# Two MLPs behind a packed attention: the early second products of batches 0 to 3 computed plainly instead of by Strassen's seven products

## The chip, the cores and the metric

The kernel runs on one core of one Trainium2 chip. The metric is the device time of one execution in microseconds (us). Of the kernel before there are three timed runs: 1403.85, 1407.91 and 1408.93 us, so a median of 1407.91 us. A fourth execution was profiled; it took 1409.86 us, 1408.0 us of them between its first and its last instruction (the span). All durations below come from that execution.

The engines are named as in the profile: PE (matrix products; PEld is its weight loading, which runs beside the products), DVE, ACT and POOL (elementwise work), SP (issues the DMA transfers).

## The reference, cut to what matters

```
p_packed = softmax(p k^T / 8) v            # 32 packed rows for each of 64 (batch, head)
x  = softmax(q p_packed^T / 8) p_packed    # 8 batches x 576 tokens x 512
g, val = x @ w_gate, x @ w_val             # 512 -> 1536
x2 = (silu(g) * val) @ w_out               # 1536 -> 512
h  = x2 @ w_in                             # 512 -> 2048
out = bend(h) @ wo2                        # h where h >= 1, 0 where h <= -1, (h + 1)^2 / 4 between
```

All values are float32. The kernel carries each operand of its large products as a high and a low float16 half, so that one product of operands is three matmuls: low by high, high by low, high by high.

## The kernel before, in words

**Units and passes.** The first MLP is cut into eight batches of 576 tokens and six pairs of blocks of its hidden dimension (a pair is 256 of the 1536 hidden columns). One batch with one pair is a *unit*. A unit's first product (`Projected.step`) is 8 steps of 6 matmuls, 48 matmuls of 288 columns; ahead of it stands its packed-row product (`make_projection`), 24 narrow matmuls that multiply the 32 packed rows of each head with the gate and value weights. ACT applies silu to a step's result, DVE multiplies the value half onto it, and the unit's hidden values then lie in a buffer `h` as four quarters (two hidden blocks by two halves of the batch's tokens). 

The order of units is fixed by `PHASES`: batch 0 with pair 0, batch 0 with pair 1, batch 1 with pairs 0 and 1, batches 0 and 1 with pair 2, batches 2 to 5 with pairs 0 to 2 each; after that pairs 3 to 5 of all eight batches, and pairs 0 to 2 of batches 6 and 7. One batch with one such group of pairs is a *pass*. The first twelve units make seven passes, those of batches 0 to 3 with pairs 0 to 2.

**The second product of a pass.** `second_strassen` multiplies the 2x2 blocks of the output weights with the 2x2 blocks of hidden values by Strassen's seven products. For that, `Projected.quarters` makes three sums and differences more and one intermediate from the four quarters and splits all seven operands into halves: four additions (three instructions), three casts to float16 and three subtractions for the low halves. Each of the seven products is done for both column groups of the output: 7 x 2 x 3 = 42 matmuls of 288 columns for a pair. The products are summed up in three PSUM banks for each group, and a bank is read after each of the seven into one of four accumulators, so there are 14 reads for a pass (`gather`, `add_to`; DVE, or ACT when the accumulator is fresh). A batch's accumulators are loaded from and stored to `sums1` in HBM between its passes. 

**Around it.** In the same stretch the kernel computes the attention, four heads of one batch at a time (a *quad*; 16 in all, in stages a, b and c), and converts the weights from float64 words (`convert_w1`, `prepare_w1`).

**What sets the order.** The kernel records every operation with its costs, its operands and the buffers it needs; `Order.run` then issues them to the engines by its own cost model, PE's in about the recorded sequence with a look ahead of 32 operations, the others by due times. On the chip each engine runs its list in that order and waits at semaphores. When a piece of attention or weight conversion is recorded is set by tables: two *places* go by in each unit, and `NEXT`, `REST` and `SPACE` name the places of quads 2 and later; `LATE` names those of the weights. `prepare(k + 1)` records the packed-row product of the next unit, at the start of unit k. There are 37 operand buffers `op` and eight PSUM banks, seven of them `ps`. Nearly every tensor operation of two inputs is recorded by one helper (`either`, L390), casts by another (`copy`, L402 to L408), every DMA by L433. Lines that the steps below speak of: L763 attention scores, L959 packed-row product, L1474 first product, L1417 second product, L1326 accumulation, L1484 silu, L1488 the value half, L647 and L652 the squares of the output weights and their sum over partitions.

## Time and profile before

| | |
|---|---|
| timed runs | 1403.85, 1407.91, 1408.93 us |
| profiled execution, its span | 1409.86 us, 1408.0 us |
| PE, PEld busy | 1339.7 us (95%), 1073.9 us (76%) |
| DVE, ACT, POOL busy | 1089.0 us (77%), 903.5 us (64%), 1092.9 us (78%) |
| unit 1 starts, unit 13 starts (first L1474 matmul) | 51.1 us, 251.9 us |
| second MLP starts (first L1205 matmul) | 718.5 us |

The busy time of PE is not its work at full speed: a matmul's span in the trace is longer than the distance to the next one when they follow closely, so a PE that is fed in bits can look busy. PEclk is the clock that PE was granted, 1.00 for 2.4 GHz; the other level is half of that.

### The profile page before, as it was taken

To read this page: it belongs to the slowest core of one execution; us is meant where nothing else is said; L and a number is where in the kernel's file an instruction comes from. 1 tells how busy PE (TensorE), PEld (TensorE's weight loads), DVE (VectorE), ACT (ScalarE), POOL (GpSimd) and SP (SyncE) were. 2 spreads that over 40 slices of the span, in tenths; PEclk is the share of its full clock that TensorE was granted. 3 is DMA by queue.
4 is the path that set the end of the run, shared out by engine and by line. 5 is a ranking of instruction groups with operands and counts; after the bars stand their busy time and mean duration, and the time that the engine had idled before them with its cause. 6 is when DMAs were issued, how large, how long until landed. Compare 5 with 4: busy or idle time off the path is not lost.

```text
span 1408.0 us, 33413 instructions
## 1 busy us (share of the span) xinstructions
PE 1339.7 (95%) x12903; PEld 1073.9 (76%) x12908; DVE 1089.0 (77%) x1985; ACT 903.5 (64%) x1663; POOL 1092.9 (78%) x936
## 2 busy tenths in 40 slices
PE   5788989899899999999999999999999999999998
PEld 2455656577576777777788888888888888888887
DVE  6998888897488887777878888777767878766774
ACT  5877776788477877777767566655545546564551
POOL 1468656678398988989998999987888979885883
PEclk8799999999999999999999999999999999999999
DMA  9865667677567777778865324352337531444312
GB/s 328 290 199 167 195 204 240 194 227 268 186 214 246 233 248 244 256 261 292 281 236 185 135 83 151 131 199 96 106 123 244 187 130 76 149 167 173 113 61 90
DMA packets 143455, 267.87 MB, mean 190 GB/s; under 512 B 15296, under 2 KB 77248, under 8 KB 143296
## 3 DMA queue, kind: packets, MB, share of 16 engines
q1 hardware_dynamic: 143296, 265.74, 56.6%
q8 instruction: 101, 1.65, 0.5%
q14 instruction: 58, 0.48, 0.1%
HBM read 168.30 MB, written 97.39 MB: 189 GB/s over the span
## 4 chain that ended last, share of the span: by engine, by line
PE 74%; POOL 3%; DVE 3%; DMA 2%; ACT 2%; issue 2%; SPq 0%; DVEq 0%; POOLq 0%; ACTq 0%
PE ps L1417 31%; PE ps L1205 20%; PE ps L1474 13%; PE cv L1417 4%; PE cv L1205 2%; PE ps L959 2%; POOL op L390 1%; DMA wsp<-raw 1%; PE ps L763 1%; DMA raw<-w2f 1%; POOL h L390 1%; POOL raw L390 1%; DVE acc L1326 0%; DMA op<-in_qT 0%; DMA raw<-in_wo 0%
## 5 line engine op out<-in xcount | busy, mean ns | idle before, releaser
L1417 PE MATMUL ps<-op,op 128*128 128x256 f16 (+1 forms) x4467 | 595.8, 279 | 19.3 <-POOL op L390 9.6
L1417 PEld LDWEIGHTS <-op 128*128 128x128 f16 x5040 | 492.1, 98 | 116.9 <-issue 29.4
L390 POOL TENSOR_TENSOR op<-h,op 128x512 f16<-128x512 f32 (+4 forms) x362 | 461.0, 1290 | 107.4 <-ACT op L402 88.1
L1474 PE MATMUL ps<-op,op 128*128 128x288 f16 x2292 | 337.7, 290 | 10.1 <-DVE t L856 2.3
L1205 PEld LDWEIGHTS <-op 128*128 128x128 f16 x3024 | 295.8, 98 | 35.2 <-issue 0.3
L1205 PE MATMUL ps<-op,op 128*128 128x256 f16 x2700 | 321.4, 273 | 0.1
L1474 PEld LDWEIGHTS <-op 128*128 128x128 f16 x2304 | 223.7, 99 | 85.9 <-issue 27.7
L402 ACT CAST op<-h 128x512 f16<-128x512 f32 (+4 forms) x370 | 216.8, 622 | 64.3 <-POOL h L390 42.2
L390 POOL TENSOR_TENSOR h<-h,h 128x512 f32<-128x512 f32 (+1 forms) x200 | 222.2, 1111 | 15.0 <-DVE h L1559 10.6
L1326 DVE SCALAR_TENSOR_TENSOR acc<-ps,g,acc 128x288 f32<-128x288 f32 (+1 forms) x198 | 118.5, 603 | 69.3 <-PE ps L1417 64.6
L1556 ACT ACTIVATE ps<-m,half,g 128x512 f32<-128x512 f32 x129 | 100.5, 779 | 62.2 <-POOL m L1553 36.1
L390 POOL TENSOR_TENSOR h<-h 128x576 f32<-128x576 f32 (+1 forms) x83 | 117.4, 1415 | 28.2 <-DVE h L1488 16.0
L404 ACT ACTIVATE lent<-ps,g 128x512 f32<-128x512 f32 x89 | 60.7, 686 | 90.1 <-PE ps L1205 78.0
L1559 DVE SCALAR_TENSOR_TENSOR h<-ps,g,h 128x512 f32<-128x512 f32 x129 | 95.1, 742 | 30.1 <-ACT ps L1556 30.0
L1553 DVE TENSOR_SCALAR m<-h,g 128x512 f32<-128x512 f32 x73 | 61.1, 837 | 49.1 <-ACT ps L1556 42.8
L390 POOL TENSOR_TENSOR raw<-raw 128x256 f32<-128x256 f32 (+1 forms) x95 | 86.4, 916 | 14.7 <-ACT raw L404 9.9
L390 POOL TENSOR_TENSOR op<-op,t 128x576 f32<-128x576 f32 x32 | 40.0, 1250 | 73.9 <-DVE kp L482 26.7
L1488 DVE SCALAR_TENSOR_TENSOR h<-ps,g,h 128x288 f32<-128x288 f32 x119 | 60.9, 512 | 45.4 <-PE ps L1474 36.1
L1188 DVE SCALAR_TENSOR_TENSOR h<-ps,g,lent 128x512 f32<-128x512 f32 x96 | 70.6, 744 | 28.5 <-PE ps L1205 22.3
L1553 POOL TENSOR_SCALAR m<-h,g 128x512 f32<-128x512 f32 x71 | 61.0, 859 | 36.9 <-DVE h L1188 19.5
L390 DVE TENSOR_TENSOR op<-h,op 128x512 f16<-128x512 f32 (+1 forms) x70 | 83.6, 1206 | 1.4 <-ACT lent L404 0.9
L1484 ACT ACTIVATE h<-ps,g 128x288 f32<-128x288 f32 x119 | 59.4, 499 | 37.6 <-PE ps L1474 37.1
(171 smaller groups left out, 1710.4 us busy)
## 6 DMA issues: line engine op xcount, KB each, us to landing
op<-wsp_out SPq DMA_DIRECT2D x44, 448.0 KB, 5.4
xsp<-op SPq DMA_DIRECT2D x36, 448.0 KB, 3.7
op<-xsp SPq DMA_DIRECT2D x36, 448.0 KB, 6.3
op<-wsp SPq DMA_DIRECT2D x32, 448.0 KB, 4.9
sums<-acc SPq DMA_DIRECT2D x88, 144.0 KB, 3.3
acc<-sums SPq DMA_DIRECT2D x88, 144.0 KB, 3.4
h<-in_w SPq DMA_DIRECT2D x24, 512.0 KB, 5.1
op<-in_kT SPq DMA_DIRECT2D x32, 288.0 KB, 4.7
```

The costliest lines, as they stand in the source:

```text
L390: lambda e: engine(e).tensor_tensor(dst(), x(), y(), op=op), r, w, late,
L402: nc.scalar.copy(dst(), src())
L404: nc.scalar.activation(dst(), src(), AF.Copy, scale=scale())
L1188: psum_dve(T, lambda: nc.vector.scalar_tensor_tensor(dst(), lanes(bank.t), self.r(), lanes(add.t), op0=ALU.mult, op1=ALU.add), [(bank, 0), ...
L1205: nc.tensor.matmul(dst, a, b, start=start, stop=stop, skip_group_check=True)
L1326: psum_dve(n, lambda: nc.vector.scalar_tensor_tensor(acc.t[:, :n], bank.t[:, :n], pw.output()(), acc.t[:, :n], op0=ALU.mult, op1=ALU.add), ...
L1417: nc.tensor.matmul(bank.t[:, l * wide:(l + 1) * wide], x, y, start=first and l == 0 and m == 0, stop=last and l == len(lefts) - 1 and m == ...
L1474: nc.tensor.matmul(bank.t[:, :H2], half(self.m[s][x])[:, cols], z_part(z2, y, t), start=(s == 0 and m == 0), stop=(s == NQUAD - 1 and m == 2),
L1488: psum_dve(H2, lambda: nc.vector.scalar_tensor_tensor(dst(), bank.t[:, :H2], self.pw.of(0, p)(), dst(), op0=ALU.mult, op1=ALU.mult), [(ban ...
L1553: o.add({"POOL": 0.85, "DVE": 0.42}, lambda e: engine(e).tensor_scalar(out=lanes(m.t), in0=dst(), scalar1=top(), scalar2=low(), op0=ALU.mi ...
L1556: act(T, lambda: nc.scalar.activation(bank.t, m.t, AF.Square, bias=half_one[:, 0:1], scale=inv()), [(m, 0), (f, 0)], [(bank, 0)], fixed=0.35)
L1559: psum_dve(T, lambda: nc.vector.scalar_tensor_tensor(dst(), lanes(bank.t), top(), dst(), op0=ALU.mult, op1=ALU.max), [(bank, 0), (h, t), ( ...
```

## The change

For the seven passes of batches 0 to 3 with pairs 0 to 2, the second product is done plainly: each of the four output blocks is the sum of two products of blocks, 8 x 2 x 3 = 48 matmuls for a pair, two lanes into one PSUM bank, which is then read once (8 reads for a pass). The hidden values are only split into halves, lane by lane as soon as a lane's values are there (`split`). The output weights of the kept pairs still get their seven Strassen operands, since other batches use them; the fourth quarter, which is none of the seven, gets halves of its own in one more `op` buffer (`fourth`, `plain_out`). The packed-row product of the second unit is recorded in the middle of the first unit and no longer at its start (`PROMPT`). Quads 13 and later come at places 30, 36, 42 and 48 instead of 34, 40, 46 and 52; the other entries of the table round to the same places as before.

```diff
+    fourth = o.buf("op")
+    def plain_out(p, raw, scale, akey):
+        base = lambda: raw.t[:, 0:4, :]
+        copy(1024, base, base, q(raw, 0, 1, 2, 3) + [akey], q(raw, 0, 1, 2, 3), scale=scale)
+        hi, lo = lambda: fourth.t[:, 2 * p, :], lambda: fourth.t[:, 2 * p + 1, :]
+        copy(N, hi, lambda: raw.t[:, 3, :], q(raw, 3), q(fourth, 2 * p))
+        either(N, lo, lambda: raw.t[:, 3, :], hi, sub, q(raw, 3) + q(fourth, 2 * p), q(fourth, 2 * p + 1), None, PREP_LO)
...
-    FIRST, EARLY = 2, 2
+    FIRST, EARLY, PROMPT = 2, 2, 1
-    NEXT, REST, SPACE, AHEAD = (0, 0.8, 2, 5.5, 8.5, 11.5, 14.5, 17.5, 20.8,23.8,26.8), 34, 6.0, 1.2
+    NEXT, REST, SPACE, AHEAD = (0, 0.8, 2, 5.5, 8.5, 11.5, 14.5, 17.5, 20.5, 23.5, 26.5), 30, 6.3, 1.2
...
+    PLAIN = [(b, pairs) for layer, pairs, blocks in PHASES for b in range(*blocks)
+             if layer == 1 and b < 4 and pairs[0] < EARLY_PAIRS]
+    def second_plain(b, span, hidden, pw):
...
+        def step(group, r, k, n, pair):
+            at = (group, r, k)
+            if n == 0:
+                banks[at] = o.buf("ps")
+            bank = banks[at]
+            terms = [
+                (weights(pair, (0, 1, 3, 2)[2 * r + lane], group), hidden[pair][2 * k + lane]) for lane in range(2)
+            ]
+            def emit():
+                for lane, (left, right) in enumerate(terms):
+                    (lh, ll), (rh, rl) = left[0](), right[0]()
+                    for m, (x, y) in enumerate(((ll, rh), (lh, rl), (lh, rh))):
+                        nc.tensor.matmul(
+                            bank.t[:, :H2], x, y, start=n == 0 and lane == 0 and m == 0,
+                            stop=n == len(pairs) - 1 and lane == 1 and m == 2,
+                        )
...
+            acc, key, cols = o.buf("acc"), ("sums1", b, group, f"c{r + 1}{k + 1}"), slice(H2 * k, H2 * k + H2)
+            if not first_of:
+                dma(0.15, lambda: acc.t[:, :H2], lambda: sums1[:, b, 2 * r + group, cols], [key], [(acc, 0)])
+            add_to(acc, bank, H2, pw, not first_of)
+            dma(0.15, lambda: sums1[:, b, 2 * r + group, cols], lambda: acc.t[:, :H2], [(acc, 0)], [key], 10.0)
...
-            if not self.queue:
+            if self.plain and t == 1:
+                self.split(lane)
+            elif not self.queue:
                 self.quarters()
+        def split(self, lane):
...
+            copy(2 * H2, dst[0], src, keys, q(hi, lane, lane + 2))
+            either(2 * H2, dst[1], src, dst[0], sub, keys + q(hi, lane, lane + 2), q(lo, lane, lane + 2), None, HIDDEN_LO)
...
-        prepare(k + 1)
+        if k >= PROMPT:
+            prepare(k + 1)
...
             if s == each // 2:
                 next_place()
+                if k < PROMPT:
+                    prepare(k + 1)
...
-        steps = second_strassen(layer, b, pairs, hidden, pw)
+        second = second_plain if layer == 1 and (b, pairs) in PLAIN else partial(second_strassen, layer)
+        steps = second(b, pairs, hidden, pw)
```

In the changed kernel's rows the lines have moved: L763 is L777 there, L808 is L822, L652 is L666, L701 is L715, L1474 is L1541, L1488 is L1555, L1326 is L1340, and L390 is L391.

**PE, up to the first unit's first product.** PE's list before the change, from the last matmuls of a weight's norm (L701) to the start of the first unit (L1474):

```order
L701 MATMUL ps_155<-raw_136,ones 128x512
L847 MATMUL ps_153<-ident,pp_168 128x128
L763 MATMUL ps_152<-op_120,ppT_164 32x288 x2
L763 MATMUL ps_152<-op_122,ppT_164 32x288 x2
L763 MATMUL ps_154<-op_120,ppT_164 32x288 x2
L763 MATMUL ps_154<-op_122,ppT_164 32x288 x2
L854 LDWEIGHTS ones
L854 MATMUL ps_149<-pp_168,ones 128x128
L652 MATMUL ps_155<-sq_87,ones_79 128x2
L808 MATMUL ps_151<-ident,op_106 128x128 x4
L1474 LDWEIGHTS op_129
L1474 MATMUL ps_152<-op_119,op_129 128x288
```

The same place in the changed kernel:

```order
L868 MATMUL ps_153<-pp_168,ones 128x128
L777 MATMUL ps_152<-op_124,pT_169 32x288 x2
L777 MATMUL ps_152<-op_127,pT_169 32x288 x2
L777 MATMUL ps_154<-op_124,pT_169 32x288 x2
L777 MATMUL ps_154<-op_127,pT_169 32x288 x2
L715 LDWEIGHTS ones
L715 MATMUL ps_151<-raw_139,ones 128x512
...
L1541 LDWEIGHTS op_130
L1541 MATMUL ps_153<-op_119,op_130 128x288
```

The sum over partitions (L652, now L666), which stood ahead of the first unit, is gone from there. It now stands between the unit's matmuls:

```order
L1541 LDWEIGHTS op_130
L1541 MATMUL ps_154<-op_121,op_130 128x288
L666 MATMUL ps_155<-sq_87,ones_79 128x2
L1541 LDWEIGHTS op_130
L1541 MATMUL ps_150<-op_119,op_130 128x288
```

The first product no longer waits behind it; 36 of the first unit's 48 matmuls now stand ahead of it.

**POOL, between two of the early units.** POOL's list before, one unit's hidden values (`h_141` into `h_143`, `op_119`), with attention's `op_109` between:

```order
L390 TENSOR_TENSOR h_143<-h_141 128x576
L390 TENSOR_TENSOR op_119<-h_141,op_118 128x576
L390 TENSOR_TENSOR op_109<-op_124,op_109 128x576
L390 TENSOR_TENSOR h_143<-h_143,h_141 128x288
L390 TENSOR_TENSOR h_143<-h_141,h_143 128x288
L390 TENSOR_TENSOR op_119<-h_143,op_118 128x1152
```

And in the changed kernel, one unit's (`h_142` into `op_112`) and the first half of the next (`h_140` into `op_101`):

```order
L391 TENSOR_TENSOR op_112<-h_142,op_130 128x2x288
L391 TENSOR_TENSOR op_102<-op_106,op_102 128x576
L391 TENSOR_TENSOR op_112<-h_142,op_130 128x2x288
L391 TENSOR_TENSOR op_101<-h_140,op_124 128x2x288
L391 TENSOR_TENSOR op_110<-op_110,t_175 128x576 x2
```

Five of POOL's instructions for a unit (a sixth, of 288 columns, is sometimes on DVE) became two, of 2 x 288 columns each.

**DVE, in a second product's results.** DVE's list before, among attention's operations, where a pass's results are read (L1326):

```order
L1326 SCALAR_TENSOR_TENSOR acc_145<-ps_153,f_159,acc_145 128x288
L1326 SCALAR_TENSOR_TENSOR acc_144<-ps_154,f_159,acc_144 128x288
L1326 SCALAR_TENSOR_TENSOR acc_145<-ps_155,f_159,acc_145 128x288
L1326 SCALAR_TENSOR_TENSOR acc_146<-ps_153,f_159,acc_146 128x288
L780 TENSOR_SCALAR t_174<-t_174 128x1
L1326 SCALAR_TENSOR_TENSOR acc_146<-ps_154,f_159,acc_146 128x288
L972 SCALAR_TENSOR_TENSOR op_104<-ps_150,kp,op_99 128x512
L1326 SCALAR_TENSOR_TENSOR acc_144<-ps_153,f_159,acc_144 128x288
L972 SCALAR_TENSOR_TENSOR op_104<-ps_149,kp,op_104 128x512
L914 TENSOR_REDUCE t_176<-op_135 128x18
L1326 SCALAR_TENSOR_TENSOR acc_147<-ps_153,f_159,acc_147 128x288
```

And in the changed kernel, in one of these passes:

```order
L1340 SCALAR_TENSOR_TENSOR acc_146<-ps_149,f_157,acc_146 128x288
L1109 SCALAR_TENSOR_TENSOR f_160<-cx_0_3_309,f_160,base_0_3_308 128x11
L1555 SCALAR_TENSOR_TENSOR h_141<-ps_155,f_158,h_141 128x288
L1112 TENSOR_SCALAR f_160<-f_160 128x11
L936 STREAM_TRANSPOSE op_124<-op_106 128x576
L1340 SCALAR_TENSOR_TENSOR acc_145<-ps_153,f_157,acc_145 128x288
L1340 SCALAR_TENSOR_TENSOR acc_147<-ps_151,f_157,acc_147 128x288
L1340 SCALAR_TENSOR_TENSOR acc_144<-ps_150,f_157,acc_144 128x288
```

Seven reads for a column group, three of the four accumulators read and written twice, became four, one for each accumulator.

Over the whole program the lists differ in this: PE has 72 matmuls more (1512 at L1417 and 576 plain ones in place of 2016); DVE has 42 accumulations fewer with four scaled copies out of PSUM more, and 11 casts and subtractions of hidden values fewer; POOL has 47 instructions fewer; ACT has four casts fewer (eight of 1152, twelve of 576 and six of 288 columns fewer, 22 of 2 x 288 more), four fresh accumulators fewer, and four more loads of its function table. The count of DMAs is the same, 958.

## Rows read from the trace of the kernel before

**Rows 1.** The page: busy time; PE and its clock in 40 slices of the span.

```profile
PE 1339.7 (95%) x12903; PEld 1073.9 (76%) x12908; DVE 1089.0 (77%) x1985; ACT 903.5 (64%) x1663; POOL 1092.9 (78%) x936
...
PE   5788989899899999999999999999999999999998
...
PEclk8799999999999999999999999999999999999999
```

**Rows 2.** Windows of the span: each engine's busy us (instructions), clock, DMA share, GB/s.

```profile
0.00:51.00 51.00, 29.64 (x292) 12.79 (x294) 39.03 (x166) 33.70 (x74) 13.63 (x19) 0.75 0.94 317
51.00:123.00 72.00, 59.16 (x639) 36.15 (x639) 65.85 (x192) 54.10 (x99) 47.26 (x40) 0.92 0.67 217
123.00:252.00 129.00, 115.90 (x1274) 79.99 (x1274) 109.01 (x257) 95.11 (x176) 80.91 (x68) 0.99 0.64 209
252.00:301.00 49.00, 45.09 (x434) 31.54 (x435) 42.73 (x95) 36.93 (x70) 33.94 (x30) 0.93 0.58 181
301.00:351.00 50.00, 50.00 (x567) 37.63 (x564) 42.16 (x88) 39.18 (x80) 37.82 (x31) 1.00 0.82 269
...
372.00:387.00 15.00, 10.67 (x89) 6.85 (x88) 5.32 (x11) 5.72 (x11) 1.03 (x1) 0.89 0.43 130
387.00:450.00 63.00, 59.90 (x649) 43.80 (x639) 53.64 (x120) 47.52 (x98) 54.75 (x49) 1.00 0.73 234
500.00:600.00 100.00, 100.00 (x974) 76.46 (x973) 80.72 (x159) 74.83 (x162) 88.84 (x77) 1.00 0.78 251
```

**Rows 3.** Chain of waits over the span: start, us, what.

```profile
711.64 4.41 PE ps L1474 x36
```

**Rows 4.** Windows of the first product's matmuls alone (L1474).

```profile
123.00:252.00 129.00, 56.57 (x385) 37.15 (x383) 0.99 0.64 209
```

**Rows 5.** Windows of the second product's matmuls alone (L1417).

```profile
123.00:252.00 129.00, 45.89 (x294) 28.38 (x294) 0.99 0.64 209
```

**Rows 6.** Groups by line and shape, 50 to 300 us: busy, mean ns, idle before, releasers.

```profile
L1474 PE MATMUL ps<-op,op 128*128 128x288 f16 x720 | 107.7, 296 | 4.5 <-DVE t L856 2.3 <-ACT op L785 1.5 <-DVE h L1488 0.3
L1417 PE MATMUL ps<-op,op 128*128 128x288 f16 x504 | 81.2, 292 | 14.3 <-POOL op L390 7.4 <-DVE acc L1326 4.2 <-ACT acc L404 1.0
...
L390 POOL TENSOR_TENSOR op<-h,op 128x1152 f16<-128x1152 f32 x14 | 33.6, 2397 | 14.4 <-ACT op L402 7.9 <-DVE t L916 3.8 <-DMA sums<-acc 2.7
L1326 DVE SCALAR_TENSOR_TENSOR acc<-ps,f,acc 128x288 f32<-128x288 f32 x66 | 32.4, 507 | 6.6 <-PE ps L1417 3.3 <-DMA acc<-sums 2.1 <-ACT acc L404 0.9
...
L390 POOL TENSOR_TENSOR h<-h,h 128x288 f32<-128x288 f32 x28 | 22.3, 795 | 0.9
...
L390 POOL TENSOR_TENSOR h<-h 128x576 f32<-128x576 f32 x14 | 19.8, 1411 | 12.4 <-DVE h L1488 10.7 <-DVE topp L860 1.3 <-DMA op<-in_kT 0.4
L390 POOL TENSOR_TENSOR op<-h,op 128x576 f16<-128x576 f32 x15 | 19.7, 1310 | 24.4 <-ACT op L402 23.3 <-DVE op L406 1.1
...
L1484 ACT ACT_TABLE_LOAD x13 | 16.7, 1283 | 3.0 <-DVE f L1098 2.7
...
L402 ACT CAST op<-h 128x1152 f16<-128x1152 f32 x12 | 13.8, 1148 | 1.8 <-POOL h L390 1.7
...
L390 DVE TENSOR_TENSOR op<-h,op 128x288 f16<-128x288 f32 x3 | 3.0, 1007 | 0.0
```

**Rows 7.** Timeline of PE before the first unit: start, us, instruction [idle before].

```profile
45.41 0.29 PE L854 MATMUL ps<-pp,ones 64*128 64x128 bf16 x1
49.74 0.58 PE L652 MATMUL ps<-sq,ones 128*128 128x2 f32 x2 [4.04 <-ACT junk L647]
...
51.07 4.04 PE L1474 MATMUL ps<-op,op 128*128 128x288 f16 x24
```

**Rows 8.** Timeline of PE at 373 us, the same columns.

```profile
373.61 0.90 PE L1474 MATMUL ps<-op,op 128*128 128x288 f16 x6 [0.59 <-ACT h L1484]
375.21 0.90 PE L1474 MATMUL ps<-op,op 128*128 128x288 f16 x6 [0.70 <-DVE h L1488]
```

**Rows 9.** Chain of waits, 150 to 300 us.

```profile
236.85 5.94 DMA op<-in_qT
```

More of the change, by code (lines that the diff above doesn't have):

```diff
@@ L2 @@
 import math
+from functools import partial
 import concourse.bass as bass
@@ L1440, in total, with weights @@
             field(lambda c=c: kx2[:, c:c + 1], lambda: topx[:, B + b:B + b + 1], [("topx2", b)], [("kx2", c)])
+    PLAIN = [(b, pairs) for layer, pairs, blocks in PHASES for b in range(*blocks)
+             if layer == 1 and b < 4 and pairs[0] < EARLY_PAIRS]
+    def second_plain(b, span, hidden, pw):
+        pairs = range(*span)
+        first_of = (1, b) not in summed
+        summed[1, b] = summed.get((1, b), 0) + len(pairs)
+        banks, accs = {}, {}
+        def weights(pair, i, group):
+            cols = slice(128 * group, 128 * group + 128)
+            if i == 3:
+                return (lambda: [fourth.t[:, 2 * pair + h, cols] for h in range(2)]), q(fourth, 2 * pair, 2 * pair + 1)
+            return part(ops[1, "out", pair], i, cols)
+        def step(group, r, k, n, pair):
[14 more added lines that the diff above has]
+                        )
+            pe(6 * MM1, emit, [x for left, right in terms for x in (*left[1], *right[1])], [(bank, 0)],
+               unit=bank, opens=n == 0)
+            if n < len(pairs) - 1:
+                return
+            acc, key, cols = o.buf("acc"), ("sums1", b, group, f"c{r + 1}{k + 1}"), slice(H2 * k, H2 * k + H2)
[3 more added lines that the diff above has]
+            dma(0.15, lambda: sums1[:, b, 2 * r + group, cols], lambda: acc.t[:, :H2], [(acc, 0)], [key], 10.0)
+        return [
+            lambda g=g, r=r, k=k, n=n, p=p: step(g, r, k, n, p)
+            for k in range(2) for g in range(2) for r in range(2) for n, p in enumerate(pairs)
+        ]
@@ L1442, in packed_attention_then_two_mlps, with __init__ @@
     class Projected:
-        def __init__(self, b, p, spare, pw, zz):
+        def __init__(self, b, p, spare, pw, zz, plain):
             self.b, self.p, self.pw, self.zz, self.m = b, p, pw, zz, made.pop((b, p))
-            self.h = o.buf("h")
+            self.h, self.plain = o.buf("h"), plain
             hi, lo = o.buf("op"), o.buf("op")
+            self.queue = [(lane, t, kind) for lane in range(LANES) for t in range(2) for kind in range(2)]
+            self.steps = len(self.queue)
+            if plain:
+                self.parts = [((hi, i), (lo, i)) for i in range(4)]
+                return
@@ L1456, in __init__ @@
             ]
-            self.queue = [(lane, t, kind) for lane in range(LANES) for t in range(2) for kind in range(2)]
-            self.steps = len(self.queue)
         def hidden(self):
@@ L1462, in of @@
                 return (lambda: [rows_of(x)[:, r, :] for x, r in self.parts[i]]), [*self.parts[i]]
-            return [of(i) for i in range(7)]
+            return [of(i) for i in range(len(self.parts))]
         def step(self):
@@ L1490, in step @@
             ), [(bank, 0), (f, 0), key], [key])
-            if not self.queue:
+            if self.plain and t == 1:
+                self.split(lane)
+            elif not self.queue:
                 self.quarters()
+        def split(self, lane):
+            h, (hi, lo) = self.h, [x for x, _ in self.parts[0]]
+            rows = slice(lane, lane + 3, 2)
+            src = lambda: four(h, H2)[:, rows, :]
+            dst = [lambda b=b: rows_of(b)[:, rows, :] for b in (hi, lo)]
+            keys = q(h, lane, lane + 2)
+            copy(2 * H2, dst[0], src, keys, q(hi, lane, lane + 2))
+            either(2 * H2, dst[1], src, dst[0], sub, keys + q(hi, lane, lane + 2), q(lo, lane, lane + 2), None, HIDDEN_LO)
         def quarters(self):
```

5 lines of the change are left out of this document (4 added, 1 removed).

## The prediction, made before the changed kernel was run

> **What bounds the kernel now.** I read the page first, then windows of the span, then the groups and waits of the first 300 us.
>
> The page says that PE is busy for 95% of the span, and its 40 slices show nines from about the twelfth on [rows 1]. The windows split the span in two. From 301 us on PE is nearly always busy (50.00 of 50 us, and 100.00 of 100 at 500 us); the exceptions that count lie at 372 to 387 us (10.67 of 15) and 387 to 450 us (59.90 of 63), 7.4 us together [rows 2]. Behind 301 us the time is therefore the count of matmuls by 0.1225 us for 288 columns (36 in 4.41 us) [rows 3], and nothing of it is changed but the places of three quads.
>
> The front, 51 to 301 us, is another matter: this is where all units with a plain product lie (unit 13, the first of batch 4, starts at 251.9 us). PE's busy time leaves 29.9 us of 250 there (72 less 59.16, 129 less 115.90, 49 less 45.09) [rows 2]. It is too kind: from 123 to 252 us PE ran 385 + 294 matmuls of 288 columns [rows 4, 5], which need 83 us at 0.1225 us, yet those two groups alone count as busy for 102 us. The weight loads show it better. Where PE never idles, at 301 us, they take 37.63 of 50 us, 75%; in the three windows of the front they take 50%, 62% and 64% [rows 2]. So PE does 67%, 82% and 86% of what it could do, and the room is 24 + 23 + 7 = 54 us.
>
> The Trainium skill states this rule, "Perfetto Trace Analysis", section "Identifying the Most-Contended Engine": PE's matmul occupancy is no good measure of how near it is to its limit, and the busy share of the weight loads is one of two to use instead. This trace agrees, with 62% against 75% [rows 2]. By matmul occupancy the room would be 29.9 us and the change could win at most some 21 us; by the weight loads it could win some 45 us.
>
> What PE waits for there: ahead of the second product it is idle for 14.3 us, 7.4 of them for POOL's halves of the hidden values, 4.2 for DVE's and 1.0 for ACT's accumulation, which keeps banks and accumulators; ahead of the first product for 4.5 us [rows 6]. The granted clock is 0.92 from 51 to 123 us and 0.93 from 252 to 301 us, so PE was at its lower level, 1.2 GHz, for part of them, each time after it had waited; that is 9 us of the room [rows 2]. DVE is the fullest of the engines that feed it: busy for 91%, 85% and 87% of the three windows, against ACT's 74 to 75% and POOL's 63 to 69% [rows 2].
>
> **The change part by part.** The base is the profiled execution, 1409.9 us (span 1408.0), 2.0 us above the median of the timed runs; I do not correct the sum for this, the range takes it in.
>
> *72 matmuls more.* Twelve units with 48 in place of 42. 72 x 0.1225 = +8.8 us, if PE had no room to take them in [rows 3].
>
> *Ahead of the first unit.* PE waited 4.04 us for ACT's squares of the output weights (L647), with the sum over partitions (L652) in front of the first unit's first product [rows 7]. After the change 36 of the unit's matmuls stand ahead of that sum. Between 0 (the wait only moves behind them) and -4 us; I take -3, since what is behind it now is a quarter of a unit and the results of the sum are wanted only by the second product's weights.
>
> *Hidden values.* For each unit POOL loses 1.411 + 2 x 0.795 + 2.397 + 1.310 = 6.7 us in five instructions and gets two of 576 elements, for which the nearest row is 1.310 us: 2.6 us [rows 6]. That is 4.1 us a unit, 49 us of POOL's 162 us in the front [rows 2]. The length of the way counts more: before, the last halves come after three dependent additions, a cast of 1.148 us and a subtraction of 2.397 us; now after one cast and one subtraction, and the first lane's are made while PE still works on the second.
>
> *Reads of PSUM.* 42 accumulations fewer on DVE, 21.3 us at 0.507 us [rows 6]; four scaled copies more, bounded by the same row, +2.0; eleven casts and subtractions fewer, at up to 1.007 us each, the dearest row of that kind, some -10 us [rows 6]. DVE loses about 29 us of its 217.6 us in the front [rows 2]. At an unchanged DVE share of 87%, the front would be 33 us shorter. A bank is also held for one step of 6 to 18 matmuls and not over a column group.
>
> *ACT* loses little: eight casts of 1.148 us and smaller ones go, 22 of 576 elements come, together about -5 us, and four table loads of 1.283 us come back, +5.1 [rows 6]. It is at 74% from 123 us on, where 78% goes with a full PE [rows 2]; if it may not go above that, those 178 us cannot get shorter than by 10 us.
>
> *The fourth quarter* costs three casts and three subtractions of 256 elements, below 0.8 us each by the 288-element row of POOL [rows 6], ahead of a second product that waits for the other weights anyway: nothing. The buffer is one of 37, and a plain unit takes a third of a buffer less: nothing. The DMAs are as many as before. *PROMPT* puts the second unit's 24 narrow matmuls later, beside the third's; they were ready in time before, between units 1 and 2, and cost the same wherever they stand: nothing, or some tenths of a microsecond each way.
>
> *What the front gives back.* Bounds: nothing, since waits for attention and its loads (one q load stands in the chain with 5.94 us [rows 9]) might set the pace anyway; or 42 us, which is what the DVE end needs to bring the front 33 us lower with the 8.8 us paid. I take 20, near the middle, and this way: 12.6 us of PE's idle has releasers that the change thins out (7.4 + 4.2 + 1.0) [rows 6]; the idle rows show only 29.9 of 54 us, so these stand for some 23; a little stays.
>
> *Behind the front.* The q, k and v loads, the scores and the softmax of quads 13 to 15 come two units earlier each. Bounds: -7.4 us, if the waits at 372 to 450 us go with them, and +10 (the second rival). I take 0.
>
> Sum: 1409.9 + 8.8 - 3 - 20 + 0 = 1395.7, so 1396 us.
>
> **The rivals.**
>
> *DVE sets the pace alone: 1384 us.* For it: DVE's share in the front, and that PE is full at 301 us with DVE at 84% [rows 2]. Against: in the first window nothing much is relieved before unit 4, since the order puts as many of DVE's operations ahead of it as before, and PE would have to run at 94% of its full rate. With the first window unchanged but for some 15 matmuls (+2), the start (-3) and 123 to 301 us shorter by DVE's relief there (151.7 us of 217.6, so 20 us, by 0.85: -24): 1409.9 + 2 - 3 - 24 = 1385; a little of the first window with it, 1384.
>
> *The gain is given back behind the front: 1406 us.* The four stages of quads 13 to 15 fall into 301 to 372 us, where PE had no room at all and DVE, ACT and POOL were at 84, 78 and 76% [rows 2]. The price is read from the next stretch: where quads and the second MLP's weights met a full PE, it lost 7.4 us [rows 2]; a third more, since now 301 to 372 us is hit too, is 10 us: 1396 + 10 = 1406. For it: those are the stages that filled the vector engines there. Against: what comes earlier is taken away later.
>
> *Banks: 1416 us, slower.* The changed order lets first and second product alternate in sixes; each six (0.735 us) closes a bank that ACT or DVE must read before it opens again. At 373 us PE did run like that: six matmuls in 0.90 us, then 0.59 and 0.70 us idle for ACT's and DVE's reads, six in about 1.5 us [rows 8]. The twelve units have 96 first sixes and up to 96 second ones; if 26 of the 192 pause for 0.75 us, the 20 us are spent again, and 1409.9 + 8.8 - 3 = 1415.7 us is left. Below 26 it does not decide. Against: there are 16 reads for a one-pair pass and its unit in place of 22, and Strassen held three banks open where now one is.
>
> **How the numbers follow.** The forecast has 0.45, with a range of its own from 1389 to 1403; the DVE pace 0.15, given back 0.22, banks 0.18. What a measurement of this kernel can tell from no change is 0.5%, 7 us: faster is below 1400.9, slower above 1414.9. Of the forecast 0.39 lies below 1400.9, with the DVE pace and 0.03 of the give-back that is 0.57; of banks 0.16 lies above; 0.27 remains for the same. The range from 1383 to 1413 leaves out half of the DVE case (0.08) and two thirds of the banks case (0.12).
>
> **What would show it.** In the profile after: PE with 576 matmuls at a new line and 72 more in all; unit 13's first product some 10 to 15 us before 251.9 us; the idle before the plain product far below 14.3 us, and POOL's halves gone as its releaser; weight loads near 70% from 123 us to unit 13, not 62%; DVE's share about as before or lower; the clock of the first 300 us nearer to 1.00. The start is right if the first L1474 comes at 47 to 48 us. Unit 13 near 240 us with the end near 1406 us would be the give-back; new waits of first and second products for ACT and DVE in 0.6 us pieces, with unit 13 at 255 us or later, would be the banks. The prediction is wrong if the front isn't shorter, or if the waits behind 301 us change by more than 7 us.

## The result, and the profile after

The changed kernel takes 1387.01 us (median of four runs, 1384.26 to 1388.30) against 1407.57 us of the kernel before on the same chips (1403.85 to 1408.93): a ratio of 0.9855, 95% interval 0.9831 to 0.9880, so 20.6 us less. The forecast was 1396 us; the time lies in the range on record, and 2 us below the range that the forecast had for itself. Its profiled execution took 1387.68 us, with a span of 1385.9 us; that execution is read below. The profiled execution of the kernel before lies 2.3 us above its median and this one 0.7 us above its own, so differences between the two traces come out some 1.6 us larger than between the timed runs.

The page of the kernel after, busy time of the engines (sum, share of the span, instructions), PE by 40 slices and its clock, answering to [rows 1]:

```profile
PE 1332.7 (96%) x12980; PEld 1077.3 (78%) x12980; DVE 1082.0 (78%) x1939; ACT 901.9 (65%) x1664; POOL 1038.5 (75%) x889
...
PE   5788999999999999999999999999999999999998
...
PEclk8799999999999999999999999999999999999999
```

PE's unbroken row of nines begins at the fifth slice, not at the twelfth. Windows of the span after, with the columns of [rows 2]:

```profile
51.00:123.00 72.00, 60.02 (x681) 40.31 (x682) 67.43 (x195) 55.09 (x107) 35.13 (x31) 0.95 0.72 234
123.00:235.00 112.00, 106.68 (x1231) 76.87 (x1230) 84.99 (x210) 86.36 (x166) 42.10 (x36) 1.00 0.72 228
235.00:283.00 48.00, 47.80 (x536) 34.46 (x541) 40.33 (x93) 38.17 (x74) 31.68 (x28) 1.00 0.69 233
...
352.00:365.00 13.00, 13.00 (x148) 9.71 (x133) 7.25 (x18) 6.51 (x12) 7.30 (x6) 1.00 0.67 212
365.00:419.00 54.00, 52.69 (x553) 37.79 (x552) 42.41 (x100) 43.32 (x82) 44.74 (x39) 1.00 0.74 241
500.00:600.00 100.00, 100.00 (x973) 76.32 (x971) 83.56 (x150) 75.76 (x160) 89.45 (x77) 1.00 0.76 244
```

The weight loads fill 56%, 69% and 72% of the three windows of the front, where it was 50%, 62% and 64%. POOL's share falls to 49% and 38% in the first two, DVE's to 76% in the second, while in the first DVE is at 94%, more than before. The granted clock is 0.95 and then 1.00. The short stretch in which PE ran in sixes with pauses (now 352 to 365 us) is full: 13.00 of 13 us, against 10.67 of 15 [rows 2, 8].

Groups by line and shape after, 50 to 300 us, with the columns of [rows 6] (L1541 is the first product, L1486 the plain one, L391 POOL's helper, L1340 the accumulation):

```profile
L1541 PE MATMUL ps<-op,op 128*128 128x288 f16 x759 | 112.8, 290 | 4.1 <-ACT h L1551 1.7 <-DVE op L986 1.5 <-ACT acc L405 0.9
L1486 PE MATMUL ps<-op,op 128*128 128x288 f16 x576 | 85.6, 287 | 2.3 <-DVE acc L1340 2.2
...
L391 POOL TENSOR_TENSOR op<-h,op 128x576 f16<-128x576 f32 x28 | 36.9, 1317 | 65.1 <-ACT op L403 49.4 <-DVE t L930 6.0 <-issue 5.2
...
L1340 DVE SCALAR_TENSOR_TENSOR acc<-ps,f,acc 128x288 f32<-128x288 f32 x26 | 12.9, 509 | 6.2 <-DMA acc<-sums 6.2
```

The idle time ahead of the second product was 14.3 us, 7.4 of them for POOL; it is 2.3 us now and POOL is no releaser of it. The mean of one matmul falls from 296 and 292 ns to 290 and 287 (PE waits less in between, and its granted clock is higher). Waits for reads of banks are the 2.2 us here, and the 1.7 and 0.9 us ahead of the first product.

Where the time went is read best from the start of each unit (every 48th matmul of the first product begins one):

| starts at, us | before | after | difference |
|---|---|---|---|
| unit 1 | 51.1 | 46.1 | -5.0 |
| unit 2 | 64.6 | 65.8 | +1.2 |
| unit 5 | 122.7 | 116.0 | -6.7 |
| unit 13 | 251.9 | 237.2 | -14.7 |
| unit 16 | 300.7 | 283.9 | -16.8 |
| unit 22 | 387.2 | 364.8 | -22.4 |
| unit 29 | 479.8 | 454.4 | -25.4 |
| second MLP | 718.5 | 695.3 | -23.2 |
| end of the span | 1408.0 | 1385.9 | -22.1 |

The start wins 5 us and has lost them by unit 2; units 2 to 13 win 15.9 us; units 13 to 29, of which none has a plain product of its own, win 10.7 us more; 3.3 us are given back behind unit 29. Of the 576 plain matmuls 144 still run behind the start of unit 13, the last at 281.8 us, so the front ends with unit 16: 2.1 of the 10.7 us come before it and 8.6 behind it.

### The profile page after: what moved, and what is told of

It is laid out like the page before. It is cut to its first block, busy times and chain, and to the rows that moved or that the text cites. A ratio compares the mean times of both kernels' runs of the same rounds, so it can differ in the third digit from the quotient of the medians.

```text
span 1385.9 us, 33438 instructions
## 1 busy us (share of the span) xinstructions
PE 1332.7 (96%) x12980; PEld 1077.3 (78%) x12980; DVE 1082.0 (78%) x1939; ACT 901.9 (65%) x1664; POOL 1038.5 (75%) x889
## 4 chain that ended last, share of the span: by engine, by line
PE 81%; DMA 6%; DVE 6%; ACT 4%; issue 2%; POOL 1%; SPq 1%; DVEq 0%; ACTq 0%; POOLq 0%
PE ps L1431 32%; PE ps L1219 19%; PE ps L1541 16%; PE ps L1486 3%; PE cv L1431 3%; PE cv L1219 2%; PE ps L973 2%; POOL op L391 1%; DMA sums<-acc 1%; DMA op<-in_qT 1%; PE ps L777 1%; DMA h<-in_wo 1%; SPq L434 1%; ACT op L403 1%; DMA acc<-sums 1%
## 5 line engine op out<-in xcount | busy, mean ns | idle before, releaser
L1431 PE MATMUL ps<-op,op 128*128 128x256 f16 (+1 forms) x4197 | 543.0, 277 | 5.5 <-POOL op L391 3.6
L391 POOL TENSOR_TENSOR op<-h,op 128x512 f16<-128x512 f32 (+4 forms) x354 | 442.1, 1265 | 139.4 <-ACT op L403 115.6
L1431 PEld LDWEIGHTS <-op 128*128 128x128 f16 x4536 | 442.6, 98 | 80.9 <-issue 5.7
L1541 PE MATMUL ps<-op,op 128*128 128x288 f16 x2262 | 332.4, 287 | 6.8 <-ACT h L1551 2.2
L1219 PEld LDWEIGHTS <-op 128*128 128x128 f16 x3024 | 295.8, 98 | 35.9 <-issue 0.9
L1219 PE MATMUL ps<-op,op 128*128 128x256 f16 x2628 | 312.2, 273 | 0.4 <-DVE h L1202 0.4
L1541 PEld LDWEIGHTS <-op 128*128 128x128 f16 x2304 | 221.9, 98 | 81.7 <-issue 26.0
L391 POOL TENSOR_TENSOR h<-h,h 128x512 f32<-128x512 f32 (+1 forms) x176 | 202.2, 1149 | 10.9 <-DVE h L1637 9.1
L1340 DVE SCALAR_TENSOR_TENSOR acc<-ps,g,acc 128x288 f32<-128x288 f32 (+1 forms) x199 | 119.1, 603 | 62.8 <-PE ps L1431 60.0
L1634 ACT ACTIVATE ps<-m,half,g 128x512 f32<-128x512 f32 x123 | 95.8, 779 | 56.8 <-POOL m L1631 37.0
L391 POOL TENSOR_TENSOR h<-h 128x576 f32<-128x576 f32 (+1 forms) x71 | 99.8, 1406 | 24.3 <-DVE h L1555 12.0
L1637 DVE SCALAR_TENSOR_TENSOR h<-ps,g,h 128x512 f32<-128x512 f32 x123 | 90.7, 742 | 26.6 <-ACT ps L1634 26.4
L391 POOL TENSOR_TENSOR raw<-raw 128x256 f32<-128x256 f32 (+1 forms) x94 | 86.0, 922 | 11.2 <-ACT raw L405 6.7
L391 POOL TENSOR_TENSOR op<-op,t 128x576 f32<-128x576 f32 x32 | 38.3, 1199 | 73.7 <-DVE kp L483 25.0
L1486 PE MATMUL ps<-op,op 128*128 128x288 f16 x576 | 85.6, 287 | 2.3 <-DVE acc L1340 2.2
L1555 DVE SCALAR_TENSOR_TENSOR h<-ps,g,h 128x288 f32<-128x288 f32 x115 | 58.6, 511 | 28.3 <-PE ps L1541 20.0
L391 DVE TENSOR_TENSOR op<-h,op 128x512 f16<-128x512 f32 (+2 forms) x66 | 79.8, 1221 | 0.2 <-ACT op L403 0.2
```

Of the source, the lines that this page charges most:

```text
L391: lambda e: engine(e).tensor_tensor(dst(), x(), y(), op=op), r, w, late,
L1219: nc.tensor.matmul(dst, a, b, start=start, stop=stop, skip_group_check=True)
L1340: psum_dve(n, lambda: nc.vector.scalar_tensor_tensor(acc.t[:, :n], bank.t[:, :n], pw.output()(), acc.t[:, :n], op0=ALU.mult, op1=ALU.add), ...
L1431: nc.tensor.matmul(bank.t[:, l * wide:(l + 1) * wide], x, y, start=first and l == 0 and m == 0, stop=last and l == len(lefts) - 1 and m == ...
L1486: nc.tensor.matmul(bank.t[:, :H2], x, y, start=n == 0 and lane == 0 and m == 0, stop=n == len(pairs) - 1 and lane == 1 and m == 2,)
L1541: nc.tensor.matmul(bank.t[:, :H2], half(self.m[s][x])[:, cols], z_part(z2, y, t), start=(s == 0 and m == 0), stop=(s == NQUAD - 1 and m == 2),
```

## The experiments

All ratios are to the kernel before on the same chip, with their 95% interval; a difference between two kernels is that of their ratios times 1406 us, and carries some 4 to 5.5 us of uncertainty, since the intervals are 2 to 4.5 us to each side. The starts of units are read from one execution of each kernel.

### The three edits by themselves

**The plain product alone**: the changed kernel with the old places.

```diff
-    FIRST, EARLY, PROMPT = 2, 2, 1
+    FIRST, EARLY, PROMPT = 2, 2, 0
-    ... 17.5, 20.5, 23.5, 26.5), 30, 6.3, 1.2
+    ... 17.5, 20.8,23.8,26.8), 34, 6.0, 1.2
```

> The plain second product of batches 0 to 3 alone; places of the quads and the second unit's packed-row product as before. Theory (the plain product relieves what feeds PE, the rest is small): most of the 20.6 us, so 1391 to 1394 us, unit 13 at 237 to 240 us. Rival (the earlier quads and the moved packed-row product bring it, the plain product only pays for its 72 matmuls): 1402 us or more.

Measured: 1391.27 us, ratio 0.9890 (0.9859 to 0.9922), 15.5 us less than before, as the theory said. Unit 13 starts at 232.6 us, 19.3 us earlier than before and earlier than the 237 to 240 us expected.

**The table alone**, on the kernel before (the last line above, the other way round). Besides quads 13 and later it moves stages b and c of quad 12, from places 30 and 34 to 28 and 30.

> Quads 13 and later earlier by four places, nothing else, on the kernel before. Theory: at most the waits behind unit 16, so 1401 to 1407 us, with unit 16 at about 300 us as before. Rival (the table brings the gain): below 1397 us.

Measured: 1402.96 us, ratio 0.9971 (0.9957 to 0.9985), 4.1 us less, give or take 2: the theory held. Unit 16 starts at 304.3 us, not at 300.

**The later packed-row product alone**, on the kernel before (`if k >= PROMPT` around `prepare(k + 1)`).

> The second unit's packed-row product recorded in the middle of the first unit, nothing else, on the kernel before. Theory: it only moves 24 narrow matmuls, 1405 to 1409 us, unit 1 at 51 us. Rival (it is what lets the first unit start at 46 us, and the 5 us stay): 1402 to 1403 us.

Measured: 1405.67 us, ratio 0.9991 (0.9974 to 1.0008): no difference that these runs can tell. The time is the theory's, the start is not: unit 1 starts at 47.4 us, and unit 2 at 64.5 us, as in the kernel before (64.6 us).

**All but the table** (the second pair of lines above).

> The changed kernel with the quads at their old places. Theory: it loses what the table brings behind unit 16, 1389 to 1395 us. Rival (the table brings the gain): 1400 us or more.

Measured: 1394.60 us, ratio 0.9906 (0.9877 to 0.9936), so the table is worth 7.2 us on top of the plain product, give or take 5.

**All but the later packed-row product** (the first pair of lines above).

> The changed kernel without the move of the second unit's packed-row product. Theory (the move lets the first unit start 3 to 5 us earlier but gives it back before unit 2 and costs 3 us more by unit 13): 1382 to 1385 us, unit 2 at 63 us, unit 13 at 233 us. Rival (the move is worth its 5 us at the start): 1389 us or more.

Measured: 1385.33 us, ratio 0.9847 (0.9830 to 0.9864). That edit brings nothing, and may cost a microsecond or two (the two kernels without the table, with and without that edit, say 2.2 us, also within the uncertainty). In this kernel unit 1 starts at 50.6 us and unit 2 at 64.2 us; with the edit, at 46.1 and 65.8 us. The timeline of PE at the start, of the kernel after (columns as in [rows 7]), says why:

```profile
45.67 0.59 PE L715 MATMUL ps<-raw,ones 128*128 128x512 bf16 x2 [1.39 <-ACT raw L418]
46.10 3.10 PE L1541 MATMUL ps<-op,op 128*128 128x288 f16 x24
49.03 0.71 PE L822 MATMUL ps<-ident,op 128*128 128x128 f32 x5
51.94 0.90 PE L842 MATMUL ps<-op,op 128*32 128x64 f32 x40 [2.19 <-DVE op L407]
...
63.06 0.40 PE L973 MATMUL ps<-op,lent 64*32 64x512 f16 x4 [2.06 <-DVE lent L887]
64.43 1.47 PE L973 MATMUL ps<-op,lent 64*32 64x512 f16 x20 [0.98 <-DVE op L986]
```

The wait for the squares (4.04 us, [rows 7]) no longer stands ahead of the unit, but half a unit later PE waits for a cast on DVE that attention needs, and just ahead of unit 2 its packed-row product (L973), moved there by the edit, waits twice more for DVE. That engine was at 94% from 51 to 123 us.

What the table removes is seen just ahead of unit 22. POOL's timeline in the kernel before, 370 to 390 us:

```profile
370.67 2.37 POOL L390 TENSOR_TENSOR op<-h,op 128x1152 f16<-128x1152 f32 x1 [1.26 <-ACT op L402]
387.81 1.16 POOL L390 TENSOR_TENSOR op<-op,t 128x576 f32<-128x576 f32 x1 [14.78 <-DVE t L789]
```

The window of the same stretch with the plain product alone (columns as in [rows 2]):

```profile
352.00:367.00 15.00, 10.20 (x95) 6.82 (x94) 6.02 (x12) 6.73 (x13) 0.46 (x1) 1.00 0.45 132
```

and with the table alone:

```profile
369.00:385.00 16.00, 15.93 (x169) 11.53 (x166) 9.12 (x23) 8.86 (x18) 7.72 (x7) 1.00 0.78 263
```

POOL stood for 14.8 us at one instruction of a quad's softmax whose other operand came late from DVE (L789), with the next unit's sums behind it in its queue, and PE had one bank at a time to run in. The plain product alone keeps that stall (PE 10.20 of 15 us); with the new places it is gone (15.93 of 16). From unit 16 to the end the profiled executions take 1107.3 us before, 1111.6 with the plain product alone and 1107.9 without the table, but 1097.6 with the table alone and 1102.0 after. Ahead of unit 16 the table alone loses 3.6 us. So the gain behind the front is the table's, and the stall that it removes is the one found; that no other wait has a part in it was not shown.

### What in the plain product pays

**Fewer matmuls**: each unit's plain product leaves out 6 of its 48 matmuls, so that PE issues no more than before the change.

```diff
                     for m, (x, y) in enumerate(((ll, rh), (lh, rl), (lh, rh))):
+                        if lane == 1 and m == 0 and (r, k) != (0, 0):
+                            continue
```

> The changed kernel with 6 of each 48 plain matmuls left out (the low half of the weights' second lane in six of eight steps), 72 in all, so that the plain product has as many as Strassen's; order of all else the same. Theory (relieved as it is, PE sets the pace from unit 6 on): 5 to 8 us off, 1379 to 1382 us. Rival (DVE sets the pace in the front, PE has room): 0 to 2 us off, 1385 to 1387 us.

Measured: 1386.17 us, ratio 0.9854 (0.9828 to 0.9881), against 0.9855: the 72 matmuls cost 0 us, give or take 5, and not 8.8. Unit 13 starts at 237.9 us and unit 16 at 284.0 us, as with them (237.2 and 283.9 us). My theory fell here, and the rival's time held; that DVE sets the pace, as the rival had it, is another matter (next run). The profiled execution is the longest of four (1391.19 us). Its window from 123 to 235 us:

```profile
123.00:235.00 112.00, 106.49 (x1206) 74.86 (x1205) 84.80 (x211) 86.53 (x167) 40.98 (x35) 0.98 0.72 228
```

PE's busy time is the same 106.5 us with fewer instructions: it waits in the gaps instead. The granted clock was lower in that execution (0.98, and 1.00 after), so a part of what fewer matmuls give may have gone into the clock; this was not separated. The Trainium skill ("Perfetto Trace Analysis", section "Identifying the Most-Contended Engine") says that matmul busy time does not tell how near PE is to its limit, and to look at the weight loads; the run agrees: PE looked 95% busy here, its weight loads took 69%, and matmuls could be had for nothing.

**The reads back**: the 42 reads of PSUM that the change saves are made again, as second accumulations onto the same sums.

```diff
             add_to(acc, bank, H2, pw, not first_of)
+            if (r, k) != (0, 0):
+                add_to(acc, bank, H2, pw, True)
```

> The changed kernel with a second read and accumulation of 42 of the 56 plain results, as many reads of PSUM as Strassen's 98; the sums are then those results twice. Theory (the reads on DVE and the banks that wait for them are the larger part of the relief): 8 to 14 us back, 1395 to 1401 us. Rival (the shorter way of the hidden values is the larger part): 0 to 5 us back, 1387 to 1392 us.

Measured: 1391.03 us, ratio 0.9887 (0.9868 to 0.9906), 4.5 us of the gain lost, give or take 4.4; the rival's 0 to 5, not the theory's 8 to 14. The trace says that even those are mostly not lost where the reads are. Window from 123 to 235 us, and PE's longest wait from 237 to 262 us:

```profile
123.00:235.00 112.00, 107.06 (x1232) 76.90 (x1231) 90.73 (x229) 84.72 (x164) 45.90 (x39) 1.00 0.73 235
```
```profile
PE ps L777 <- DMA op<-in_qT: 3.4, 2, 2.1
```

DVE is busy for 90.73 us where it was 84.99, and PE does as much as after (107.06 and 106.68 us). Unit 13 starts at 238.2 us, 1.0 us later than after. The time goes from unit 13 to unit 16 (54.0 us, 46.7 after), where few of the added reads are left and PE waits for two q loads. From unit 5 to unit 13 DVE does 7.8 us more than after (99.59 and 91.79 us) in 0.7 us more: it doesn't set the pace there.

**The hidden sums back**: in each plain unit Strassen's sums, casts and low halves are made again, and nothing reads them.

```diff
                 self.split(lane)
+                if lane == 1:
+                    self.idle_sums()    # the additions, cast and subtraction of quarters()
```

> The changed kernel with Strassen's sums of hidden values, their casts and their low halves made again for the plain units, but nothing waits for them: the load without the way. Theory (POOL has room in the front, the load is not what PE waited for): 0 to 4 us back, 1387 to 1391 us. Rival (the load itself on POOL, DVE and ACT is the relief): 8 us or more back, 1395 us or more.

Measured: 1396.57 us, ratio 0.9924 (0.9907 to 0.9941), 9.7 us lost, although no matmul waits for those values: the rival's time. Together with the reads this is 14.2 us, near the 15.5 that the plain product brings alone, which looks as if the change had got rid of work, and the wait for its result counted little. The traces don't bear that out. Times between starts of units, us:

| | before | after | reads back | hidden sums back | sums, no cast (below) |
|---|---|---|---|---|---|
| unit 2 to 5 | 58.1 | 50.2 | 49.7 | 50.4 | 53.5 |
| unit 5 to 11 | 95.2 | 89.9 | 91.7 | 91.3 | 85.4 |
| unit 11 to 13 | 34.0 | 31.3 | 30.2 | 37.1 | 42.0 |
| unit 13 to 16 | 48.8 | 46.7 | 54.0 | 49.7 | 46.2 |
| unit 16 to the end | 1107.3 | 1102.0 | 1099.0 | 1101.6 | 1100.4 |

The largest gain lies between units 2 and 5, and there the hidden sums cost nothing when they are put back, although POOL is then as busy as before the change (48.94 us from 51 to 123 us, 47.26 before [rows 2]); the 3.3 us that the kernel of the last column loses there are back by unit 11. The window with the hidden sums back:

```profile
51.00:123.00 72.00, 63.08 (x675) 41.52 (x677) 68.59 (x195) 55.32 (x108) 48.94 (x43) 0.91 0.67 217
```

The reads cost nothing there either, but DVE does less of its other work in that run and stretch (46.98 us in all, 47.79 after), so it is no test of DVE. What is left as the cause is the shorter way of the hidden values, and less work on DVE (52.74 us in the kernel before); no run separates these two, and none puts both loads back. What the two runs lose, they lose later, and much of it at single waits.

**Its parts**: of what the last edit added, the three additions and a subtraction alone, then the cast alone.

```diff
+        def idle_sums(self):    # idle_pool
+            combined(2 * n, ..., sub, ...)       # 576 elements
+            combined(n, ..., add, ...)           # 288
+            combined(n, ..., sub, ...)           # 288
+            combined(3 * n, dst, src, src, sub, q(s, 1, 2, 3), q(spare, 1))
...
+        def idle_sums(self):    # idle_cast
+            copy(3 * n, lambda: rows_of(spare)[:, 0:3, :], lambda: four(h, n)[:, 1:4, :], ...)
```

> The changed kernel, and of what hidden_back added in each plain unit only the three additions of Strassen's hidden sums and one subtraction of 864 elements, on POOL or DVE, with no cast on ACT; nothing reads them. hidden_back cost about 9.7 us over the changed kernel (1396.6 against 1387). Theory: the load on POOL (77.5 us busy from 123 to 235 us, against 42.1) is what costs, because the plain units' own low halves queue behind it: 1394 to 1397 us here, and under 1390 us for idle_cast. Rival: it was ACT's casts, since PE's longest wait in hidden_back (5.5 us) was for a cast on ACT: 1386 to 1390 us here.

Measured: 1398.55 us, ratio 0.9944 (0.9925 to 0.9964), 12.5 us lost, 1.6 us more than the theory's range and well above the rival's. That it is more than the whole of the last edit cost is within the uncertainty.

> The changed kernel, and of what hidden_back added in each plain unit only the cast of 864 elements on ACT; nothing reads it. Twelve casts of some 1.15 us, 14 us of ACT in the front. Theory (POOL's load costs): 1386 to 1390 us. Rival (ACT's casts cost): 1392 to 1396 us. Both in parts, if the two add up: about 1391 us here and in idle_pool.

Measured: 1385.95 us, ratio 0.9861 (0.9841 to 0.9882): nothing lost, give or take 4.5. The theory held. Windows from 123 to 235 us, first with the sums, then with the cast:

```profile
123.00:235.00 112.00, 102.90 (x1169) 74.56 (x1167) 87.70 (x200) 81.08 (x157) 79.93 (x66) 0.95 0.71 226
```
```profile
123.00:235.00 112.00, 106.47 (x1198) 73.66 (x1196) 87.71 (x204) 84.65 (x163) 42.17 (x33) 1.00 0.71 229
```

POOL's load is the one thing that differs much (79.93 against 42.17 us), and even so POOL is idle for 29% of the window. How such a load costs PE time is seen in the kernel with the sums at 221 us. Its profiled execution is the shortest of five (1394.61 us), 6.9 us above that of the kernel after, and all of that is lost there: unit 11 starts at 204.2 us, 1.7 us earlier than after, and unit 13 at 246.2 us, 9.0 us later. Where the median execution loses the rest is not shown. PE, POOL and ACT there, in that order:

```profile
219.64 1.64 PE L1541 MATMUL ps<-op,op 128*128 128x288 f16 x12
229.49 1.45 PE L842 MATMUL ps<-op,op 128*32 128x64 f32 x40 [8.21 <-ACT op L403]
```
```profile
214.63 1.16 POOL L391 TENSOR_TENSOR op<-op,t 128x576 f32<-128x576 f32 x1 [4.67 <-ACT raw L458]
215.75 1.29 POOL L391 TENSOR_TENSOR op<-h,op 128x576 f16<-128x576 f32 x1
217.08 1.41 POOL L391 TENSOR_TENSOR h<-h 128x576 f32<-128x576 f32 x1
218.45 1.28 POOL L391 TENSOR_TENSOR op<-op,op 128x576 f16<-128x576 f32 x1
219.69 1.27 POOL L391 TENSOR_TENSOR op<-h,op 128x576 f16<-128x576 f32 x1
220.93 1.24 POOL L391 TENSOR_TENSOR h<-h,h 128x288 f32<-128x288 f32 x1
222.13 0.72 POOL L391 TENSOR_TENSOR raw<-raw 128x256 f32<-128x256 f32 x1
222.82 1.63 POOL L391 TENSOR_TENSOR op<-raw,op 128x768 f16<-128x768 f32 x1
224.42 2.31 POOL L391 TENSOR_TENSOR raw<-raw 128x256 f32<-128x256 f32 x3
226.69 2.13 POOL L391 TENSOR_TENSOR op<-h 128x864 f16<-128x864 f32 x1
```
```profile
225.85 0.62 ACT L403 CAST op<-raw 128x512 f16<-128x512 f32 x1 [1.20 <-POOL raw L391]
226.76 1.06 ACT L418 ACTIVATE raw<-raw 128x1024 bf16<-128x1024 f32 x1 [0.30 <-DVE raw L477]
227.73 0.60 ACT L403 CAST op<-raw 128x512 f16<-128x512 f32 x1
228.85 0.74 ACT L403 COPY op<-ps 128x512 f32<-128x512 f32 x2 [0.52 <-POOL op L391]
```

PE needs the copies that ACT makes at 228.85 us of transposed attention values. They stand in ACT's queue behind casts of weights (`raw`), which wait for POOL's weight sums, which stand in POOL's queue behind hidden work, three of the added instructions among it (217.08, 220.93, 226.69 us: 4.8 us). The copy then waits once more (0.52 us), for the buffer that it writes. That is not the whole of it, though: in the kernel after, the same copies stand ahead of those casts in ACT's list.

```profile
218.93 0.73 ACT L403 COPY op<-ps 128x512 f32<-128x512 f32 x2
```

POOL's weight sums begin at 222.13 us here and at 221.01 us there, only 1.1 us apart. So the added instructions changed the order in which the kernel issues its work, and by these rows most of the 8.21 us comes from the later place of the copies, and less from POOL's backlog. With all of the hidden work back the same copies stand behind two of the casts, and PE waits 5.49 us for them. The issue order of ACT and of POOL, with buffer numbers, shows the same buffer in both:

```
L403 COPY op7_106<-ps5_154 128x512
L391 TENSOR_TENSOR op7_106<-h2_142 128x864
```

So the added subtraction, which nobody reads, holds the buffer until 228.82 us, and the copies cannot be issued before it; that this is why they come so late in the list is likely, but not tested. Another limit: the added sums also take a second of the four `h` buffers, into which the float64 words of the weights are loaded, and the cast takes none. Whether POOL's time, the buffers or the changed order weighs most was not separated.

### How many batches

**Batches 0 and 1 only, and batches 0 to 5**, both without the later packed-row product.

```diff
-             if layer == 1 and b < 4 and pairs[0] < EARLY_PAIRS]
+             if layer == 1 and b < 2 and pairs[0] < EARLY_PAIRS]    # or b < 6
```

> no_prompt (1385.3 us) with only batches 0 and 1 taking their first pass without Strassen. table_only, with none, took 1403.0. Theory: the relief counts by the unit, and batches 0 and 1 hold half of the twelve: 1392 to 1396 us. Rival: the front's first 120 us, where DVE stays at 94%, gives back what it wins, and the gain comes from batches 2 and 3: 1398 to 1403 us.

Measured: 1387.53 us, ratio 0.9871 (0.9845 to 0.9897).

> no_prompt (1385.3 us) with batches 4 and 5 taking their first pass without Strassen too: 36 matmuls more, six units relieved. Theory: from 235 us to unit 19 PE still loses a few us to waits, and relief of POOL and DVE is worth more there than 36 matmuls at 0.1225 us (4.4 us): 1378 to 1384 us. Rival: with the change PE has hardly any room left there (weight loads at 72% of the time against 75% with a full PE), so most of the 4.4 us is paid: 1385 to 1390 us.

Measured: 1384.28 us, ratio 0.9847 (0.9822 to 0.9873).

With none, two, four and six batches the ratios are 0.9971, 0.9871, 0.9847 and 0.9847. The first six units bring 14 us, the next six about 3 (within the uncertainty), the last six nothing that can be told from zero. Neither expectation for two batches held: I had the gain spread over the units, or late. It is early. From unit 2 to unit 5 the kernel with the table alone takes 61.0 us (63.6 to 124.6), with two batches 50.5 us (63.2 to 113.7), so 10.5 of the 14 us are won before 125 us. Windows of that stretch, of the kernel before and of the kernel after:

```profile
64.60:122.70 58.10, 47.27 (x491) 29.11 (x488) 52.74 (x143) 43.47 (x82) 43.12 (x37) 0.91 0.61 195
```
```profile
65.80:116.00 50.20, 42.85 (x480) 29.20 (x476) 47.79 (x131) 38.30 (x75) 26.80 (x26) 0.98 0.71 226
```

The same 29 us of weight loads lie in 50 us and no longer in 58; POOL's share falls from 74% to 53%, DVE's rises from 91% to 95%. DVE's work falls by 5 us (52.74 to 47.79) and the stretch by 8, with DVE's share up: less work on DVE can be a part of it, but not all. At the other end, batches 4 and 5 show a full PE; the window of the kernel with six batches:

```profile
235.00:283.00 48.00, 48.00 (x548) 35.87 (x541) 42.26 (x101) 37.81 (x72) 20.39 (x18) 1.00 0.69 232
```

Weight loads at 75%, as where PE never idles [rows 2], and POOL at 42%: so it may be that what is relieved there, nobody waits for, and that the added matmuls use up what is left; the two were not separated. The kernel with six batches and that with four are the fastest that ran, and equal (both 0.9847).

## Why the prediction was right, and where it was not

**The direction and the mechanism** held: PE had room behind its busy row, and the plain product gave back about as much of it as forecast. The signs came as said: weight loads 69% from 123 us on (said: near 70), unit 13 at 237.2 us (said: 10 to 15 us before 251.9; it was 14.7), the idle before the plain product 2.3 us with POOL gone as releaser, the clock at 1.00 from 123 us.

**The 72 matmuls, +8.8**, were mis-sized: taken out, they give back 0 us, give or take 5. The step priced them at the distance of matmuls in a full PE [rows 3] in a stretch that the same text had found to be 14 to 33% short of full. "If PE had no room" was its condition, and it wasn't met.

**The front's 20 us** were about right. From unit 2 to unit 16 the kernel after wins 18.0 us, that without the table 20.4, the plain product alone 22.0. For the whole front the sum on record had +8.8 - 3 - 20 = -14.2 us, and the trace shows -16.8 at unit 16: the matmuls 8.8 too dear, the waits 2.0 too large, the start 4.2 too good. That these nearly cancel is luck. Of the parts, the reads were given 5.2 us of named waits (4.2 + 1.0, [rows 6]); put back, they cost 1.0 us by unit 13. The sentence that "the length of the way counts more" than POOL's load fits units 2 to 5, where POOL's load put back costs nothing. Further on it is not borne out: the two kernels with hidden sums back lose 6 to 11 us between units 11 and 13 with the short way kept, in a chain through POOL's and ACT's lists that the prediction did not have.

**The start, -3**, came as -5 at unit 1 and was +1.2 at unit 2; the run without that edit is as fast. The step looked at the wait it removed and not at what PE needs half a unit later, which came no sooner. And the 24 narrow matmuls, said to "cost the same wherever they stand", waited 3.0 us for DVE at their new place.

**Behind the front, 0**, is the step that failed. The sum began at a profiled execution, 1409.9 us, and lies 8.0 us above the profiled one after (1387.7 us): 2.6 us of that are the front's and 5.3 us lie behind it. The bound of -7.4 us, "if the waits at 372 to 450 us go", was on record, and the table measures near it: 7.2 us, give or take 5, with the plain product, and 4.1 us alone. The profile had the evidence [rows 2, 8]: a stretch of 15 us with POOL busy for 1.03 us is a queue that stands still, and asking what POOL waited for would have named the late quad that the edit moves. The sign of being wrong, "if the waits behind 301 us change by more than 7 us", came close: from unit 16 on the kernel after is 5.3 us shorter.

**The rivals.** DVE as the pace: its price said that nothing is won in the first window, and there, with DVE at 95%, most was won; and with the reads put back DVE did 7.8 us more from unit 5 to unit 13 in 0.7 us more. Between units 2 and 5 it may have a part. The give-back is 3.3 us behind unit 29, not 10, and not at 301 to 372 us. Banks: the 26 pauses of 0.75 us are not there; the first and second product wait for ACT's and DVE's reads for 4.8 us in all (1.7 + 0.9 + 2.2).

## What to carry to other kernels

Price an added instruction by the room of its engine in that stretch: in a PE whose weight loads stand below the share of a full stretch, matmuls may be free. What they cost in a full one, no run here shows by itself. Work that nobody waits for can still cost as much as a wait when it stands in an in-order queue ahead of something that another queue needs; a busy share of 70% is no proof against it. An experiment that puts work back also changes the order of issue: before its cost is called the price of that work, look where in the trace it is lost. Where an engine is nearly idle in a stretch in which PE stutters, look up what its next instruction waits for before putting the change of an order table at nothing.

## What the runs showed that was not expected

Unread work of 38 us on POOL from 123 to 235 us (79.93 less 42.10), with POOL at 71% there, cost 12.5 us of the kernel's time (in the profiled execution 6.9 us, in one place), while a cast of 0.9 us for each of the same units on the fuller ACT (76%) cost nothing measurable. And six of the twelve units bring most of the gain: the change counted where DVE was fullest and PE emptiest, and not by the unit.
